# Linear attention, gated feed-forward and residual: more of gate and value in seven half products, attention two blocks ahead

## The chip, the cores and the metric

The kernel runs on one core of a Trainium2 chip. The metric is the device time of one execution in microseconds. TensorE is called PE below, VectorE DVE, ScalarE ACT, GpSimd POOL; SyncE (SP) and POOL issue the transfers.

## The reference

Eight batches of 576 tokens, eight heads of 64. Attention is linear: `kv` is a 64 x 64 matrix per head, and each output row is divided by its root mean square. Its result `x` (4608 x 512) goes through a gated feed-forward layer of 1536 features and is added back under a sigmoid gate.

```python
def _attn_ref(q, k, v, g_norm):
    kv = np.einsum('bhsd,bhse->bhde', k, v)
    out = np.einsum('bhsd,bhde->bhse', q, kv)
    rms = np.sqrt(np.mean(out * out, axis=-1, keepdims=True) + 1e-06)
    return (out / rms * g_norm)

def _moe_ref(x, w_gate, w_val, w_out, w_res):
    gelu = exact_gelu(x @ w_gate)              # written with erf
    ffn_out = gelu * (x @ w_val) @ w_out
    res_gate = 1.0 / (1.0 + np.exp(-(x @ w_res)))
    return x + res_gate * ffn_out
```

## The kernel before

The tokens are worked in nine blocks of 512: blocks 0 to 7 are the first 512 tokens of a batch each, block 8 the remaining 64 of all eight. A block on PE is: gate and value for 12 tiles of 128 features ("slots" 0 to 11), the residual gate (`rps`, 16 matmuls of 512 columns), and the output product, which from block 1 on is done as seven half products (Winograd's form of Strassen's scheme) instead of eight: sums of quarters of `hid` and `w_out` are formed once, seven products of half size are accumulated in PSUM banks A, D, E and F, and some additions put the quarters together. Attention of the next batch is interleaved with the slots.

Gate and value in the plain form, one tile of 128 features: eight matmuls of 512 columns, a GELU on ACT, a product on DVE.

```python
def m_act(blk, f, gps, vps):
    ge = moep.tile([P, NJ * P], FP16, tag="ge", name="ge")
    nc.scalar.activation(out=ge, in_=gps, func=AF.Gelu)
    nc.vector.tensor_tensor(out=hids[blk][:, f, :], in0=ge, in1=vps, op=ALU.mult)

def m_gval(blk, f, pool=pmoe, tag="mm"):
    ...
    m_mm(gps, wg_c, f, blk, 0, NJ)      # four matmuls, 128x512
    m_mm(vps, wv_c, f, blk, 0, NJ)      # four matmuls
    m_act(blk, f, gps, vps)
```

Blocks 7 and 8 have gate and value in sevens too, in three groups of four tiles (`GF = 4`). `gv_group` runs a list of words: a digit is a half product of four matmuls of 256 columns, `E` an ACT copy that seeds bank E from A, `d` an ACT copy of F that is kept, `F` and `c` DVE additions of A and the kept part, `gNN` a GELU and `hNN` the product of a quarter (DVE; quarter 22 on POOL):

```python
for word in """1g 1v Eg 5g Ev 5v dg 6g dv 6v Fg 2g Fv 2v 7g g11 7v cg 3g cv 3v
               h11 g22 4g g12 h12 * 4v g21 h22 h21""".split():
```

It needs four sums of weight quarters for each of gate and value in a group (`weight_sums`), and four sums of token quarters of `xT` per block (`token_sums`), all on DVE. The weight sums are made in blocks 3 to 6, the token sums of blocks 7 and 8 in the output stage of the block before.

The output stage (cut). `aside(...)` marks places where other work may be put in ahead of a product:

```python
def first_two():
    prod(w["A"], a_of(blk, 1, 1), b_of(1, 1), True)
    nc.scalar.copy(out=w["E"], in_=w["A"])
    prod(w["D"], s_[0], wo_t[:, 0], True)
    nc.scalar.copy(out=w["d"], in_=w["D"])
    for j in range(NJ):
        m_sigmoid(j)

def others():
    prod(w["A"], s_[1], wo_t[:, 1], False)
    aside("F")
    sub(nc.vector, w["F"], w["A"], w["d"], ALU.add)
    aside("00")
    prod(w["E"], a_of(blk, 1, 2), b_of(2, 1), False)
    pf((0, 0), w["E"])
    aside("22")
    prod(w["A"], s_[2], wo_t[:, 2], False)
    sub(nc.vector, c22, w["A"], w["d"], ALU.add)
    aside("01")
    prod(w["F"], s_[3], b_of(2, 2), False)
    pf((0, 1), w["F"])                  # pf: DVE, sigmoid times sum
    fin((0, 0))                         # fin: POOL, plus x
    aside("11")
    prod(w["A"], a_of(blk, 2, 2), wo_t[:, 3], False)
    pf((1, 1), c22); pf((1, 0), w["A"])
    ...                                 # more fin, and the stores
```

Attention of a batch b, in short: `by_token` puts q in order (a copy of 128x2048), `d_qT` transposes it by DMA, `a_kv` multiplies k by v (40 small matmuls and a copy), `a_o` makes the output in four banks, `a_rem_o` that of the remaining 64 tokens of two batches (for b = 2, 3, 5, 7), `a_ss` squares on ACT and sums on DVE, `a_norm` makes the inverse root by three Newton steps, `a_t` scales, `a_x` multiplies by g, `d_xT` transposes by DMA. `load_behind` has POOL issue the loads of the next batch after a one-element copy (`hold`) that waits for a transpose. The norm:

```python
def a_norm(b, j0, j1):
    nc.vector.tensor_scalar(out=m, in0=ss, scalar1=1.0 / D, scalar2=RMS_EPS, op0=ALU.mult, op1=ALU.add)
    nc.vector.tensor_scalar(out=yy.bitcast(I32), in0=m.bitcast(I32), ...)
    nc.vector.tensor_scalar(out=mh, in0=m, scalar1=-0.5, scalar2=None, op0=ALU.mult)
    for _ in range(3):
        nc.vector.tensor_tensor(out=a, in0=yy, in1=yy, op=ALU.mult)
        nc.vector.tensor_tensor(out=a, in0=a, in1=mh, op=ALU.mult)
        nc.vector.scalar_tensor_tensor(out=yy, in0=a, scalar=1.5, in1=yy, op0=ALU.add, op1=ALU.mult)
```

Attention of batch b is done in block b - 1 (its q is put in order at the end of block b - 2).

Of the kernel before, what the change touches and what calls it, by code (L numbers as in the profile page):

```python
# [18 lines left out]
def kernel(  # L19
# [91 lines left out]
    def tiles_16(b):  # L111
        b16_t[b, "q"] = qkvp.tile([P, NJ, H, D], FP16, tag="q16", name="q16")
        by_head = [P, H, NJ * D] if b > 0 else [P, NJ, H, D]
        b16_t[b, "k"] = qkvp.tile(by_head, FP16, tag="k16", name="k16")
        b16_t[b, "v"] = qkvp.tile([P, H, NJ * D], FP16, tag="v16", name="v16")
# [10 lines left out]

    def by_token(b):
        nc.vector.tensor_copy(
            out=b16_t[b, "q"].rearrange("p j h d -> p h j d"),
            in_=raw[b, "q"].rearrange("p h (j d) -> p h j d", j=NJ),  # L130
        )
# [66 lines left out]

    def a_kv(b):
        k16 = b16_t[b, "k"]  # L200
        v16 = b16_t[b, "v"]
        kl, vl = last_kv[b % 2]
        ps = pattn.tile([P, NP, D], FP32, tag="at", name="kvp")
        for pr in range(NP):
            for j in range(NJ + 1):
                for e in range(2):
                    h = 2 * pr + e
                    nc.tensor.matmul(  # L208
                        ps[halves(e), pr, :],
                        lhsT=k16[:, h, j * D : (j + 1) * D] if j < NJ else kl[:, h, :],  # L210
                        rhs=v16[:, h, j * D : (j + 1) * D] if j < NJ else vl[:, h, :],
                        start=(j == 0),
                        stop=(j == NJ),
                    )
        nc.vector.tensor_copy(out=st[b]["kv2"], in_=ps)

# [47 lines left out]

    def a_norm(b, j0, j1):

        s = st[b]
        if "rinv" not in s:
            s["rinv"] = attnp.tile([P, NJ + 1, H], FP32, tag="ny", name="ny")
        ss, yy = (t[:, j0:j1, :].rearrange("p j h -> p (j h)") for t in (s["ss"], s["rinv"]))  # L270
        n = (j1 - j0) * H
        m = attnp.tile([P, (NJ + 1) * H], FP32, tag="nm", name="nm")[:, 0:n]
        a = attnp.tile([P, (NJ + 1) * H], FP32, tag="na", name="na")[:, 0:n]
        mh = attnp.tile([P, (NJ + 1) * H], FP32, tag="nh", name="nh")[:, 0:n]
        nc.vector.tensor_scalar(out=m, in0=ss, scalar1=1.0 / D, scalar2=RMS_EPS, op0=ALU.mult, op1=ALU.add)
        nc.vector.tensor_scalar(
            out=yy.bitcast(I32), in0=m.bitcast(I32), scalar1=-0.5, scalar2=float(0x5F3759DF), op0=ALU.mult, op1=ALU.add
        )
        nc.vector.tensor_scalar(out=mh, in0=m, scalar1=-0.5, scalar2=None, op0=ALU.mult)
        for _ in range(3):  # L280
            nc.vector.tensor_tensor(out=a, in0=yy, in1=yy, op=ALU.mult)
            nc.vector.tensor_tensor(out=a, in0=a, in1=mh, op=ALU.mult)
            nc.vector.scalar_tensor_tensor(out=yy, in0=a, scalar=1.5, in1=yy, op0=ALU.add, op1=ALU.mult)

# [176 lines left out]
    def out_by_products(blk, later, banks, amid):  # L461
# [11 lines left out]
        def first_two():  # L473
            for n in ("D", "E", "F", "A"):
                w[n] = pmoe.tile([P, 2, CH], FP32, name="w" + n, bank=banks[n])
            w["d"] = finp.tile([P, 2, CH], FP32, tag="wd", bufs=1, name="wd")
            prod(w["A"], a_of(blk, 1, 1), b_of(1, 1), True)
            nc.scalar.copy(out=w["E"], in_=w["A"])
            prod(w["D"], s_[0], wo_t[:, 0], True)
            nc.scalar.copy(out=w["d"], in_=w["D"])  # L480
            for j in range(NJ):
                m_sigmoid(j)
# [138 lines left out]
    def weight_sums(unit, eng):  # L621
# [4 lines left out]
        def one(s_, x, y, op):  # L626
            if s_ == 0:
                pool, tag = (wpool, f"ws{n}{g}") if g < 2 else (qkvp, "q16")
                gv_sums[unit] = pool.tile([P, 4, 2, 2, P], FP16, tag=tag, name="ws")
# [18 lines left out]
    def token_sums(blk, eng):  # L648
        def one(i, x, y):
            if i == 0:  # L650
                x_sums[blk] = stage.tile([P, 4, 2, 2, P], FP16, tag="qraw", name="ts")
            t = x_sums[blk]
# [9 lines left out]

    def gv_group(blk, g, banks, amid=()):

        if g == 0:
            hids[blk] = hidp.tile([P, NF, NJ * P], FP16, tag="hid", name="hid")
# [63 lines left out]

        for word in """1g 1v Eg 5g Ev 5v dg 6g dv 6v Fg 2g Fv 2v 7g g11 7v cg 3g cv 3v h11 g22 4g g12 h12 * 4v g21 h22 h21""".split():
            if word == "*":
                for f in amid:
                    f()
            elif word[0].isdigit():
                product(int(word[0]), word[1])
# [6 lines left out]
            elif word[0] == "g":  # L743
                gelu(word[1:])
            else:
                hidden(word[1:])

    def out_by_f(blk):
# [338 lines left out]

    def load_behind(b):

        nc.gpsimd.tensor_copy(out=hold, in_=st[b]["qT"][0:1, 0, 0, 0:1])  # L1090
        if pair(b) is not None:
            nc.gpsimd.tensor_copy(out=hold, in_=st[b]["qrT"][0:1, 0, 0:1])
        load_batch(b + 1)

    def at(blk, slot, *fs):
        plans[blk].setdefault(slot, []).extend(fs)

    def plan_attn(b):
# [11 lines left out]
        else:  # L1110
            if b == 3:
                amid_out[m - 1] = {"22": [lambda: by_token(b), *begin]}
            else:
# [19 lines left out]
        last = [lambda: a_t(b, NJ), lambda: a_x(b, NJ), lambda: d_xT(b, NJ, NJ + 1)]  # L1133
        if rem and b + 1 == B:
            amid_out.setdefault(m, {})["F"] = last
        elif rem:
            at(m, NF + 3, *last)

    units = [(n, g) for g in range(NF // GF) for n in "gv"]
    all_sums = [f for u in units for f in weight_sums(u, nc.vector)]  # L1140
    sums_in = {3: all_sums[0:5], 4: all_sums[5:10], 5: all_sums[10:16], 6: all_sums[16:24]}
    SUM_SLOTS = (0, 0, 1, 2, 2, 5, 5, 6)
    out_at = {}

    def banks_of(blk):

        if blk == LAST[0]:
            w = out_at[blk - 1]
            first = {"g": (w["D"], w["F"], w["E"], w["A"]), "v": [w[j] for j in range(NJ)]}
        else:  # L1150
            w = out_at[LAST[0]]
            first = {"g": (w[0], w[2], w["D"], w["A"]), "v": (w[1], w[3], w["E"], w["F"])}
        groups = []
        for g in range(NF // GF):
            groups.append({})
            for u, (a0, e, f, a1) in first.items():
                if g % 2:
                    a0, e, f = a1, f, e
                groups[g].update({(u, "A"): a0, (u, "E"): e, (u, "F"): f})
        (ga0, ge_, gf, ga1), (va0, ve, vf, va1) = first["g"], first["v"]  # L1160
        out_at[blk] = {0: ga1, 1: va1, 2: ge_, 3: ve}
        if blk == LAST[0]:
            out_at[blk].update(A=gf, D=vf, E=ga0, F=va0)
        else:
            out_at[blk].update(A=(gf, vf), D=ga0, E=va0, F=ga1)
        return groups

    late = []
    for blk in range(B + 1):
        plan = plans[blk]  # L1170
        if blk == 0:
# [5 lines left out]
            for b in range(2, B):  # L1177
                plan_attn(b)
            plan[5] = [lambda j=j: a_x(0, j) for j in range(NJ)]
        else:  # L1180
            slots = [lambda f=f: m_gval(blk, f) for f in range(NF)]
            sevens = blk in LAST
            if sevens:
                slots = [None] * NF
                ends = banks_of(blk)
                mid = [lambda: s_begin(blk)]
                for g in range(NF // GF):
                    slots[GF * g] = lambda g=g: gv_group(blk, g, ends[g], mid if g == 2 else ())
            if blk == 1:
# [3 lines left out]
            slots += [lambda i=i: outs[i]() for i in range(4 if blk < B else 2)]  # L1193
            if not sevens:
                plan.setdefault(NFH + 2, []).insert(0, lambda: s_begin(blk))
            for j, f in enumerate(sums_in.get(blk, ())):
                plan.setdefault(SUM_SLOTS[j], []).append(f)
            if blk + 1 in LAST:
                for ahead_of, f in zip(("00", "01", "22", "11"), token_sums(blk + 1, nc.vector)):
                    amid_out.setdefault(blk, {}).setdefault(ahead_of, []).append(f)  # L1200

            def products(blk=blk, outs=outs):
                s_rest(blk)
                if blk not in LAST:
                    out_at[blk] = banks_behind()
                if blk + 1 == LAST[0]:
                    out_at[blk].update({j: pattn.turn[j] for j in range(NJ)})
                if blk < B:
# [11 lines left out]
        if blk == 0:  # L1220
            new_block(1)
            more, rows = attn_plan_1()
            for i, fs in more.items():
                plan.setdefault(i, []).extend(fs)
        elif blk + 1 < B:
            new_block(blk + 1)
# [43 lines left out]
```

## Time and profile before

| | |
|---|---|
| time, median of 3 | 335.93 us (335.91 to 335.99) |
| span of the profiled execution | 334.7 us |
| granted TensorE clock | 0.999 |
| plain tile of gate or value, 4 matmuls of 512 | 0.86 us |
| half product of gate or value, 4 matmuls of 256 | 0.44 us |
| half product of the output stage, 12 matmuls of 256 | 1.31 us |
| block 3, 4, 5, 6 | 34.89, 35.29, 34.88, 35.30 us |
| block 7 (sevens, no attention) | 30.97 us |

Busy time is the time in which an engine has an instruction at work; it can include waiting that the record doesn't separate. In the chain of waits, each row is a start, a duration and the work that held the end at that moment. In the timelines, a row is an instruction or a run of equal ones; a bracket says how long the engine was idle before it and what ended the idleness. The records of successive DVE operations overlap by a little under 0.1 us, so the spacing of starts is shorter than the durations.

### The profile page before, as it was taken

How to read it: one execution, taken by the hardware profiler on the slowest of the kernel's cores; microseconds unless marked ns; L12 is line 12 of the kernel's file. 1: busy time of each engine (PE TensorE's matmuls, PEld its weight loads, DVE VectorE, ACT ScalarE, POOL GpSimd, SP SyncE). 2: the span in 40 equal slices, each digit the busy share in tenths (PEclk: the TensorE clock that was granted, in tenths of full speed). 3: DMA queues.
4: the chain of work that ended last, by engine and by line, in shares of the span. 5: the costliest groups of instructions: out<-in, count | busy, mean ns of one | idle time of the engine just before them, and what ended most of it. 6: DMA issues, size and time to landing. Idle time of an engine off the chain costs nothing.

```text
span 334.7 us, 6522 instructions
## 1 busy us (share of the span) xinstructions
PE 326.6 (98%) x2576; PEld 201.4 (60%) x2576; DVE 253.5 (76%) x498; ACT 161.5 (48%) x290; POOL 109.3 (33%) x127
## 2 busy tenths in 40 slices
PE   8999999999999999999999999999999999999993
PEld 3554454445844485447644664467445888788872
DVE  6755459579867979697778978795799877687754
ACT  3663474374336352636173525343544376646660
POOL 2882242980064018200830066004100241142232
PEclk9999999999999999999999999999999999999999
DMA  7999999689589284965496349935201330011004
GB/s 258 314 204 203 195 203 159 163 122 132 98 130 206 65 127 131 167 58 108 158 151 67 63 127 179 114 63 102 107 0 20 60 126 2 2 63 66 0 2 125
DMA packets 76688, 38.82 MB, mean 116 GB/s; under 512 B 42098, under 2 KB 74354, under 8 KB 76658
## 3 DMA queue, kind: packets, MB, share of 16 engines
q0 software_dynamic: 38752, 17.17, 40.9%
q1 hardware_dynamic: 37328, 20.71, 23.6%
q10 hardware_dynamic: 578, 0.52, 0.5%
q8 instruction: 20, 0.33, 0.4%
q14 instruction: 10, 0.08, 0.1%
HBM read 38.80 MB, written 9.44 MB: 144 GB/s over the span
## 4 chain that ended last, share of the span: by engine, by line
PE 96%; DVE 2%; issue 0%; DVEq 0%
PE gps L357 22%; PE vps L357 21%; PE wA L452 11%; PE rps L377 9%; PE fps L394 3%; PE Av L692 3%; PE Ag L692 3%; PE wF L452 3%; PE wE L452 3%; PE wD L452 3%; PE w L452 2%; PE idle L858 2%; PE kvp L208 2%; PE Fv L692 2%; PE Fg L692 2%; PE op L226 1%
## 5 line engine op out<-in xcount | busy, mean ns | idle before, releaser
L345 ACT ACTIVATE ge<-gps 128x512 f16<-128x512 f32 x84 | 50.0, 598 | 97.4 <-PE gps L357 96.4
L357 PE MATMUL gps<-xT,wg 128*128 128x512 f16 x328 | 84.3, 380 | 0.0
L357 PE MATMUL vps<-xT,wv 128*128 128x512 f16 x328 | 84.2, 379 | 0.0
L346 DVE TENSOR_TENSOR hid<-ge,vps 128x512 f16<-128x512 f16 x84 | 57.3, 684 | 33.0 <-PE vps L357 30.9
L492 POOL TENSOR_TENSOR osb<-osb,t 128x512 f32<-128x512 f32 x28 | 35.2, 1275 | 136.5 <-DVE osb L488 136.1
L357 PEld LDWEIGHTS <-wv 128*128 128x128 f16 x328 | 32.1, 98 | 38.7
L357 PEld LDWEIGHTS <-wg 128*128 128x128 f16 x328 | 30.7, 98 | 34.6 <-issue 0.2
L452 PEld LDWEIGHTS <-hid_s 128*128 128x128 f16 x384 | 37.6, 98 | 4.5 <-issue 0.2
L377 PE MATMUL rps<-wr,xT 128*128 128x512 f16 x144 | 32.5, 379 | 0.0
L452 PEld LDWEIGHTS <-hid 128*128 128x128 f16 x288 | 28.1, 98 | 5.2 <-issue 0.6
L386 ACT ACTIVATE th<-rps 128x512 f32<-128x512 f32 x36 | 21.5, 598 | 16.4 <-PE rps L377 16.4
L377 PEld LDWEIGHTS <-xT 128*128 128x128 f16 x144 | 14.1, 98 | 16.5
L245 DVE TENSOR_REDUCE ss<-sq 128x8 f32<-128x512 f32 x32 | 20.6, 680 | 2.9 <-ACT sq L243 2.7
L452 PE MATMUL wA<-wo_ts,hid_s 128*128 128x256 f16 x168 | 20.6, 272 | 0.0
L692 PEld LDWEIGHTS <-ws 128*128 128x128 f16 x192 | 18.8, 98 | 2.2
L391 ACT ACTIVATE th<-th 128x512 f32<-128x512 f32 x36 | 19.9, 622 | 0.0
L303 DVE TENSOR_TENSOR t<-op,ny 128x512 f16<-128x512 f32 x28 | 17.9, 684 | 0.1
L243 ACT ACTIVATE sq<-op 128x512 f32<-128x512 f32 x28 | 15.3, 596 | 4.5 <-PE op L226 4.1
L425 DVE TENSOR_TENSOR hid_s<-hid 128x1536 f16<-128x1536 f16 x16 | 15.3, 954 | 0.2
L317 DVE TENSOR_TENSOR t<-t,g 128x512 f16<-128x512 f16 x36 | 15.0, 468 | 0.1
L729 POOL TENSOR_TENSOR hid<-ge,c 128x512 f16<-128x512 f16 x6 | 7.0, 1166 | 23.4 <-ACT ge L723 23.4
L394 PE MATMUL fps<-wo,hid 128*128 128x512 f16 x48 | 11.2, 379 | 0.0
(173 smaller groups left out, 472.8 us busy)
## 6 DMA issues: line engine op xcount, KB each, us to landing
out_dram<-osb SPq DMA_DIRECT2D x14, 512.0 KB, 2.6
qraw<-in_q_dram POOLq DMA_DIRECT2D x7, 512.0 KB, 8.3
k<-in_k_dram POOLq DMA_DIRECT2D x7, 512.0 KB, 9.7
v<-in_v_dram POOLq DMA_DIRECT2D x7, 512.0 KB, 11.9
wg<-in_moe_w_gate_dram POOLq DMA_DIRECT2D x2, 512.0 KB, 8.3
wv<-in_moe_w_val_dram POOLq DMA_DIRECT2D x2, 512.0 KB, 8.7
wo<-in_moe_w_out_dram POOLq DMA_DIRECT2D x2, 512.0 KB, 13.7
out_dram<-osb SPq DMA_DIRECT2D x4, 256.0 KB, 2.8
```

The lines of the kernel that those rows point to most:

```text
L245: nc.vector.tensor_reduce(out=out_, in_=sq, op=ALU.add, axis=mybir.AxisListType.X)
L303: nc.vector.tensor_tensor(out=t, in0=o, in1=scale, op=ALU.mult)
L345: nc.scalar.activation(out=ge, in_=gps, func=AF.Gelu)
L346: nc.vector.tensor_tensor(out=hids[blk][:, f, :], in0=ge, in1=vps, op=ALU.mult)
L357: nc.tensor.matmul(ps[:, j0 * P : j1 * P], lhsT=w[:, cc, :], rhs=xT_t[blk][:, j0:j1, cc, :], start=(cc == 0 and j0 == 0), stop=(cc == NP - ...
L377: nc.tensor.matmul(rps, lhsT=xT_t[blk][:, j, cc, :], rhs=wr16[:, cc, :], start=(cc == 0), stop=(cc == NP - 1),)
L386: nc.scalar.activation(out=th, in_=rps, func=AF.Tanh, scale=0.5)
L391: nc.scalar.activation(out=th, in_=th, func=AF.Copy, scale=0.5, bias=0.5)
L394: nc.tensor.matmul(fps, lhsT=hids[blk][:, f, j * P : (j + 1) * P], rhs=wo16[:, f, :], start=(f == 0), stop=(f == NF - 1))
L452: nc.tensor.matmul(ps[:, e - es[0], :], lhsT=a[:, f, e * P : (e + 1) * P], rhs=b[:, f, :], start=(start and e == es[0] and f == 0), stop=( ...
L492: nc.gpsimd.tensor_tensor(out=res_all[of], in0=res_all[of], in1=t_t[blk][of], op=ALU.add)
L692: nc.tensor.matmul(out_[:, r, :], lhsT=lhsT, rhs=rhs, start=(first and r == 0 and c == 0), stop=(c == 1), skip_group_check=True,)
```

## The change

In blocks 3 to 6 the last two of the three groups of gate and value (tiles 4 to 11) are done in sevens, and the first stays plain. Its purpose is to take one product in eight out of two thirds of these blocks' gate and value work on PE. What has to move for it:

- Attention of batches 4 to 7 goes two blocks ahead, so that its work is spread over the end of one block and the plain group of the next, and so that banks of PSUM are free for the groups.
- q's copy and kv's copy go from DVE to ACT, and the norm of these batches to POOL, where each Newton step has four operations for three (fifteen in all for twelve).
- The weight sums of groups 1 and 2 are made in block 0, and those of group 0 in block 6 (blocks 7 and 8 need them). Token sums are made for blocks 3 to 8.
- The banks that gate and value use rotate with those of attention (`banks_of`).

The diff, cut to its core:

```diff
-    def by_token(b):
-        nc.vector.tensor_copy(
+    def by_token(b, copy=nc.vector.tensor_copy, js=slice(0, NJ)):
+        copy(
...
-    def a_norm(b, j0, j1):
+    def a_norm(b, j0, j1, eng=nc.vector):
...
-            nc.vector.scalar_tensor_tensor(out=yy, in0=a, scalar=1.5, in1=yy, op0=ALU.add, op1=ALU.mult)
+            if eng is nc.vector:
+                eng.scalar_tensor_tensor(out=yy, in0=a, scalar=1.5, in1=yy, op0=ALU.add, op1=ALU.mult)
+            else:
+                eng.tensor_scalar(out=a, in0=a, scalar1=1.5, scalar2=None, op0=ALU.add)
+                eng.tensor_tensor(out=yy, in0=a, in1=yy, op=ALU.mult)
...
             nc.scalar.copy(out=w["E"], in_=w["A"])
+            aside("D")
             prod(w["D"], s_[0], wo_t[:, 0], True)
             nc.scalar.copy(out=w["d"], in_=w["D"])
+            aside("gates")
...
-    def load_behind(b):
+    def load_behind(b, x_of=None):
         nc.gpsimd.tensor_copy(out=hold, in_=st[b]["qT"][0:1, 0, 0, 0:1])
+        if x_of is not None:
+            nc.gpsimd.tensor_copy(out=hold, in_=xT_t[x_of][0:1, 0, 0, 0:1])
...
+    GROUPS = {blk: (1, 2) for blk in range(3, B - 1)} | {B - 1: (1, 0, 2), B: (0, 1, 2)}
+    def plan_attn_ahead(b):
+        rem = pair(b) is not None
+        m = b - 2
+        act, pool = nc.scalar.copy, nc.gpsimd
...
+        if m in GROUPS:
+            for i in range(2):
+                at(m, 2 + i, lambda i=i: by_token(b, act, slice(2 * i, 2 * i + 2)))
+            at(m, 3, *begin)
+            if b + 1 < B:
+                at(m, 2 * GF, lambda: load_behind(b))
+            at_word(m, 1, "5v", lambda: a_kv(b, act))
+        else:
+            at(m, 5, lambda: by_token(b, act, slice(0, 2)))
+            at(m, 6, lambda: by_token(b, act, slice(2, 4)))
+            at(m, 7, *begin)
+            at(m, NF - 1, lambda: a_kv(b, act))
+            at(m, NF, lambda: load_behind(b, b - 1))
+        if rem:
+            at_word(m, 1, "h21", lambda: a_rem_o(b))
+        at(m, NF, lambda: a_o(b), lambda: a_ss(b, 0), lambda: a_ss(b, 1))
+        aside_out(m, "D", lambda: a_ss(b, 2), lambda: a_ss(b, 3))
+        aside_out(m, "gates", *[lambda: a_ss(b, NJ)] * rem, lambda: a_norm(b, 0, NJ + rem, pool))
+        at(m, NF + 3, lambda: new_block(b), lambda: a_t(b, 0), lambda: a_t(b, 1))
+        for j in range(2, NJ + rem):
+            at(m + 1, j - 2, lambda j=j: a_t(b, j))
+        for j in range(NJ):
+            at(m + 1, 2 + j // 2, lambda j=j: a_x(b, j))
+        at(m + 1, 3, lambda: d_xT(b, 0, NJ))
+        if rem:
+            at(m + 1, 3, lambda: a_x(b, NJ), lambda: d_xT(b, NJ, NJ + 1))
+
+    units = [(n, g) for g in (1, 2, 0) for n in "gv"]
+    sums = {u: weight_sums(u, nc.vector) for u in units}
+    for slot, u in ((6, ("g", 1)), (8, ("v", 1)), (11, ("g", 2)), (13, ("v", 2))):
+        for i in range(2):
+            at(0, slot + i, *sums[u][2 * i : 2 * i + 2])
+    late_sums = [f for u in (("g", 0), ("v", 0)) for f in sums[u]]
+    at(B - 2, NF + 1, *late_sums[0:4])
+    for key, f in zip(("00", "22", "01", "11"), late_sums[4:8]):
+        aside_out(B - 2, key, f)
+    for blk in GROUPS:
+        t = token_sums(blk, nc.vector)
+        if blk - 1 in GROUPS and blk < B:
+            at(blk - 1, NF + 1, *t)
+        else:
+            for key, f in zip(("00", "01", "22", "11"), t):
+                aside_out(blk - 1, key, f)
...
```

## The prediction

> **What bounds the kernel now.** I read the page's busy shares first, then the busy time by block, then the chain of waits, and then the timelines of VectorE (DVE) and GpSimd (POOL) around two transitions. The shares say that TensorE (PE) never rests:
>
> ```profile
> PE 326.6 (98%) x2576; PEld 201.4 (60%) x2576; DVE 253.5 (76%) x498; ACT 161.5 (48%) x290; POOL 109.3 (33%) x127
> ```
>
> By block (3, 4, 5, 6 and 7 in turn; the columns are length, then busy time of each engine with its instructions):
>
> ```profile
> 126.95:161.84 34.89, 34.89 (x270) 20.27 (x268) 29.11 (x61) 14.87 (x26) 10.44 (x12) 1.00 0.75 120
> 161.84:197.13 35.29, 35.29 (x285) 20.36 (x284) 28.00 (x58) 16.08 (x29) 10.19 (x13) 1.00 0.67 111
> 197.13:232.01 34.88, 34.88 (x270) 20.26 (x268) 29.02 (x57) 14.87 (x26) 10.55 (x12) 1.00 0.73 120
> 232.01:267.31 35.30, 35.30 (x287) 20.40 (x285) 30.23 (x63) 16.07 (x29) 5.04 (x5) 1.00 0.17 49
> 267.31:298.28 30.97, 30.97 (x271) 26.23 (x269) 23.35 (x36) 18.41 (x34) 8.33 (x8) 1.00 0.09 35
> ```
>
> PE's busy time is the whole of every block: there is no wait to remove, only PE work. Block 7 already has gate and value in seven half products and no attention, and VectorE works 23 of its 31 us. The chain gives the price of both forms:
>
> ```profile
> 21.49 0.86 PE gps L357 x4
> 22.35 0.86 PE vps L357 x4
> ...
> 267.31 0.44 PE Ag L692 x4
> 267.75 0.44 PE Av L692 x4
> ...
> 285.65 3.45 PE rps L377 x16
> ```
>
> A plain tile of 128 features costs 0.864 for gate and 0.864 for value: four tiles are 6.91 us. Block 7's three groups in sevens run from 267.31 to 285.65, 18.34 us, so 6.11 each. One changed group saves 0.80 us.
>
> **What the Trainium skill says.** "TensorE: Matmul & The Clock Gate", Back-to-back issue gap, has 518 cycles for 512 columns and 262 for 256 in its table; at its 2.4 GHz I estimate 216 and 109 ns. The trace agrees: 0.864/4 is 216 ns, and a 256-column matmul takes 0.437/4, 109 ns. Half products thus lose almost nothing by being smaller. (The 131 ns for N=512 in the same section isn't seen here.) "SBUF — State Buffer", Who interferes with whom, says that a VectorE operation with both inputs in SBUF and a GpSimd operation that reads SBUF exclude each other for a whole instruction. The trace agrees: the gated product of two SBUF tiles took 1.65 us at 297.94, beside a POOL addition from 297.77 to 299.04, and 0.68 us at 231.34. "PSUM — Partial Sum Buffer", PSUM bank collisions raise a hardware error, wants engines kept apart by bank: so a product that accumulates into bank A starts only when VectorE has read A. The wait lists have no PE entry for it; after the change there may be one.
>
> **The change part by part.** (1) *Sevens.* Four blocks of two groups, eight groups: each drops 32 matmuls of 512 columns and adds 56 of 256, in all 192 matmuls more. 8 x 0.80 = 6.4 us off the path. The floor is 335.9 - 6.4 = 329.5.
>
> (2) *VectorE.* A group in sevens costs it four additions and three products, about 0.69 each, 4.8 us; four plain products cost 4 x 0.684 = 2.7. Eight times 2.1 is +16.6. Token sums for four more blocks: 16 x 0.435 = +7.0. Gone: four norms of 12 small operations (about 2.3 each, -9.2), four casts of q (0.69 each, -2.7) and of kv (0.42, -1.7). Net +10, so about 263 us. The weight sums only move, two thirds of them to block 0, where the waits on "PE vps" show VectorE idle 1.0 us per tile; the last eight go into block 6.
>
> (3) *ScalarE (ACT).* A group goes from 4 x 0.60 to eight operations of 0.57 to 0.63, +2.4, in all +19. The q copies, two of 1024 elements per batch, cost 1.02 us each (by the row of 128x1024, 1019 ns), +8; kv +1.5. About 190 us, off the path.
>
> (4) *POOL.* One product of 1.17 per group, +9.4, and four norms of 15 dependent small operations. The page has only the 1x1 copies, 0.18 to 0.25 us; I estimate 0.3 for 32 to 40 elements from these and the 1.2 us of 512 elements, 4.5 us a norm, +18. About 137 us.
>
> (5) *Attention two blocks ahead.* The same PE work at other places: block 2 carries two batches (1.5 us more), block 6 none. PE sum unchanged.
>
> **Where the gain leaks.** PE ends a block's output stage by a chain through VectorE. Before, the addition into F has slack; here it is in block 7, with the VectorE operation ahead of it:
>
> ```profile
> 289.49 0.96 DVE L425 TENSOR_TENSOR hid_s<-hid,hid_s 128x1536 f16<-128x1536 f16 x1
> 293.14 0.70 DVE L425 TENSOR_TENSOR wF<-wA,wd 128x512 f32<-128x512 f32 x1 [2.70 <-PE wA L452]
> ```
>
> The group ended at 285.65, so VectorE is free 4.75 us later (290.4). The changed order puts ahead of that addition five sums of squares in blocks 3 and 5 (four in block 4) and four token sums. The timelines show starts 0.60 apart for operations that read 0.68, and 0.34 to 0.45 for token sums: 3.0 + 1.6, so the addition starts at 9.35 and has read bank A at 10.0. PE wants A for the fifth product at 0.38 (remainder rows) + 3.45 (gate) + 0.69 (output of attention) + 4 x 1.31 = 9.76. A wait of some 0.3 in blocks 3 and 5, 0.1 in block 4. In block 6, eight weight sums of half size (about 0.23 each) and the token sums delay it to about 8.8 against 8.7 (0.15), and further weight sums sit ahead of the later read of A, beside POOL's additions with their lock: another 0.6. Sum of the four output stages: 1.45.
>
> Block 3's start is worse. In block 2, POOL's loads now wait for the transpose of block 3's activations as well:
>
> ```profile
> 117.12 2.00 SPq L334 DMA_TRANSPOSE xT<-t  x1
> ...
> 130.98 0.93 POOL L120 DMA_DIRECT2D qraw<-in_q_dram  x1
> 131.90 0.89 POOL L121 DMA_DIRECT2D k<-in_k_dram  x1
> 132.78 0.90 POOL L122 DMA_DIRECT2D v<-in_v_dram  x1
> ```
>
> That transpose starts at 117.1 and lands 4.5 later (median of its row), 121.7. Two copies and six load issues (130.98 to 135.72 in this instance, 4.7 us) take POOL to 127.0; the norm behind them ends at 131.5. Block 3 starts on PE at 126.95 + 1.5 = 128.5, and VectorE's first operation there, the scaling of attention, waits for that norm; the first hidden product sits behind two scalings and ends at 133.4. PE needs its bank for the third value tile at 128.5 + 4.32 = 132.8. A wait of 0.6, and about 0.4 more where `t` times `g` meets POOL's late additions: 1.0. In blocks 4 to 6 POOL starts the norm at 9.4 after the group end and ends near 13.9; the scaling comes at about 15, so no wait.
>
> Last, the copy of kv on ACT between the seed and the kept sums of the third group: kv is ready about 3.3 into the group, the copy takes 0.4, the two kept sums then end at 4.85, and the two VectorE additions after them at 5.7; PE wants the second at 5.5. 0.15 in three blocks, 0.4 together.
>
> Sum: 329.5 + 1.45 + 1.0 + 0.4 = 332.4. I take 332.2.
>
> **The rivals.** *A: all is hidden.* PE runs through and the time is 329.6. For it: block 7 has sevens with no PE wait and VectorE has 7 us to spare there. Against: blocks 3 to 5 add attention's 8 or 9 us to that. *B: VectorE becomes the bound.* By rows, a changed block with remainder has 2.7 (plain) + 9.6 (groups) + 3.8 (hidden sums) + 4.1 (output) + 3.4 (squares) + 3.4 (scalings) + 2.2 (`g`) + 1.7 (token sums) = 30.9, of 33.3 that PE needs. By the starts' spacing it is nearer 28. On average it fits, but if waits on POOL or port locks cost 2 us a block the whole gain goes: 335 to 337. *C: GpSimd's norm is slow.* At 0.5 us for a small operation a norm takes 7.5 us: block 3's start loses 3 us more and blocks 4 to 6 begin to lose 1 to 2 each: 337 to 340. "GPSIMD Engine Reference", 3.1 Elementwise, has GpSimd at about 1.96 times VectorE's time; the trace has 1.16 to 1.27 against 0.68, about 1.8, and VectorE's small ones at 0.18 to 0.20 would give 0.35: so C isn't likely at its full size. *D: transfers come late.* Batch 4's q was issued at 95.06 with 6.0 us to land, and ACT reads it at about 104: hidden.
>
> **Range and chances.** The floor is firm, since PE's work is counted: under 329.5 nothing is to be had, and 2% (329.2) lies just beyond it, so faster by 2% has 0.02. My leaks could be zero or twice as big, and B or C in part add 2 or 3 us: 330.0 to 335.2. Slower by 2% (342.6) would need 13 us of waits, 0.03.
>
> **What would show it right or wrong.** Right: PE busy falls by about 6.4 us with 2768 matmuls; new PE idle or stretched pieces of 0.1 to 0.7 at the fifth product of the output stages and about 1 us in block 3's second or third tile; VectorE near 263, ACT 190, POOL 137 us; block 7 still 31.0. Wrong: a seven group longer than 6.2 without a wait, POOL's small operations far from 0.3, PE waiting for ACT in the groups, or VectorE without gaps through blocks 3 to 5.

## The result, and the profile after

The changed kernel takes 333.09 us (333.05 to 333.13) where the kernel before takes 335.96 us (335.91 to 336.47) beside it: a ratio of 0.9911, with a 95% interval of 0.9894 to 0.9928. It is faster by 2.9 us of the 6.4 us of matmuls that it leaves out. The question for the experiments is where the other 3.5 us went.

The page's busy shares, as before:

```profile
PE 320.6 (97%) x2768; PEld 219.6 (66%) x2768; DVE 258.7 (78%) x482; ACT 184.6 (56%) x334; POOL 133.9 (40%) x196
```

PE has the 2768 matmuls that were counted. It is busy for 6.0 us less, and no longer for the whole span. By block (3, 4, 5, 6 and 7 in turn, from each block's first gate matmul; after the length come the busy times of PE, its weight loads, VectorE, ScalarE and GpSimd, then the granted clock, the DMA share and GB/s):

```profile
128.46:163.65 35.19, 34.13 (x335) 25.05 (x333) 27.61 (x46) 21.89 (x40) 18.87 (x37) 1.00 1.05 146
163.65:197.10 33.45, 33.45 (x319) 24.93 (x317) 27.74 (x47) 20.62 (x37) 16.87 (x30) 1.00 0.71 120
197.10:231.56 34.46, 33.97 (x335) 25.05 (x333) 27.68 (x46) 21.90 (x40) 10.96 (x21) 1.00 0.31 68
231.56:263.68 32.12, 31.93 (x247) 23.85 (x245) 28.78 (x58) 16.56 (x30) 9.10 (x11) 1.00 0.19 54
263.68:294.64 30.96, 30.96 (x271) 26.22 (x268) 23.50 (x37) 18.39 (x34) 8.24 (x8) 1.00 0.09 35
```

Length minus PE's busy time is 1.06, 0.00, 0.49, 0.19 and 0.00 us: the new waits are in blocks 3, 5 and 6. VectorE has at least 3 us free in every block, also in those. PE's timeline names the waits (start, duration, instructions, and in the bracket the idle time before them and what ended it):

```profile
91.22 1.04 PE L361 MATMUL gps<-xT,wg 128*128 128x512 f16 x4 [0.33 <-DMA xT<-t]
...
124.54 1.47 PE L456 MATMUL wA<-wo_ts,hid_s 128*128 128x256 f16 x12 [0.30 <-DVE wF L429]
...
131.92 1.03 PE L361 MATMUL gps<-xT,wg 128*128 128x512 f16 x4
133.80 1.02 PE L361 MATMUL vps<-xT,wv 128*128 128x512 f16 x4 [0.86 <-DVE hid L350]
...
146.85 0.60 PE L698 MATMUL Ag<-ts,ws 128*128 128x256 f16 x4
147.45 0.60 PE L698 MATMUL Av<-ts,ws 128*128 128x256 f16 x4
...
158.05 1.47 PE L456 MATMUL wE<-wo,hid 128*128 128x256 f16 x12
159.72 1.47 PE L456 MATMUL wA<-wo_ts,hid_s 128*128 128x256 f16 x12 [0.20 <-DVE wF L429]
...
227.63 1.47 PE L456 MATMUL wA<-wo_ts,hid_s 128*128 128x256 f16 x12 [0.49 <-DVE wF L429]
262.37 1.47 PE L456 MATMUL wA<-wo_ts,hid 128*128 128x256 f16 x12 [0.19 <-DVE osb L429]
```

The brackets must not be taken for the loss. Four 256-column matmuls read 0.60 us, but the next four start 0.43 or 0.44 later: the recorded end lies 0.16 us behind the moment at which the next could begin. A delay therefore costs its bracket plus 0.16, and a short one has no bracket at all: from 146.85 to 147.45 the spacing is 0.60 where 0.44 is due, and nothing shows; a delay of 0.27 us in run 10 shows nothing either. In what follows a *loss* is the spacing of two starts minus the number of matmuls times 216 ns (512 columns) or 109 ns (256 columns). For 131.92 to 133.80 it is 1.88 - 0.86 = 1.02 us.

Added up over blocks 2 to 6 (the joints with attention's small matmuls, about 0.1 each and present before too, are left out). The fifth of the seven output products is the one with `s_[2]`; it can go into bank A only when the addition into F has read it. In block 6 the loss is at the seventh.

| place | predicted | before | after |
|---|---|---|---|
| block 2, first gate tile (transfer of its activations) | none | 0.06 | 0.50 |
| block 2, fifth output product | none | 0 | 0.47 |
| block 3, start | 1.0 | 0 | 1.02 |
| kv copy, blocks 3, 4 and 5 | 0.4 | 0 | 0.46 |
| block 3, fifth output product | 0.3 | 0 | 0.36 |
| block 4, fifth output product | 0.1 | 0 | 0 |
| block 5, fifth output product | 0.3 | 0 | 0.66 |
| block 6, output stage | 0.75 | 0 | 0.36 |
| sum | 2.85 | 0.06 | 3.83 |

335.96 - 6.4 + 3.77 = 333.3, within 0.3 us of the measured time. The six named places give 2.86 us; block 2 was named nowhere and gives 0.91 more. For comparison, the fifth product of block 2 in the kernel before follows the fourth at 1.31 us:

```profile
121.55 1.47 PE L452 MATMUL wE<-wo,hid 128*128 128x256 f16 x12
122.86 1.47 PE L452 MATMUL wA<-wo_ts,hid_s 128*128 128x256 f16 x12
```

### The profile page after: what moved, and what is told of

It is laid out like the page before. It is cut to its first block, busy times and chain, and to the rows that moved or that the text cites. A ratio compares the mean times of both kernels' runs of the same rounds, so it can differ in the third digit from the quotient of the medians.

```text
span 331.3 us, 7035 instructions
## 1 busy us (share of the span) xinstructions
PE 320.6 (97%) x2768; PEld 219.6 (66%) x2768; DVE 258.7 (78%) x482; ACT 184.6 (56%) x334; POOL 133.9 (40%) x196
## 4 chain that ended last, share of the span: by engine, by line
PE 88%; DVE 4%; DMA 3%; SPq 1%; ACT 1%; issue 1%; POOL 0%; DVEq 0%; ACTq 0%
PE vps L361 13%; PE gps L361 13%; PE rps L381 10%; PE wA L456 9%; PE Av L698 8%; PE Ag L698 7%; PE Fv L698 4%; PE Fg L698 4%; PE fps L398 3%; PE w L456 2%; PE wD L456 2%; PE wF L456 2%; PE wE L456 2%; PE Ev L698 2%; PE Eg L698 2%; PE kvp L208 2%
## 5 line engine op out<-in xcount | busy, mean ns | idle before, releaser
L349 ACT ACTIVATE ge<-gps 128x512 f16<-128x512 f32 x52 | 30.8, 597 | 64.6 <-PE gps L361 64.3
L361 PE MATMUL vps<-xT,wv 128*128 128x512 f16 x200 | 51.3, 379 | 0.9 <-DVE hid L350 0.9
L361 PE MATMUL gps<-xT,wg 128*128 128x512 f16 x200 | 51.4, 379 | 0.3 <-DMA xT<-t 0.3
L350 DVE TENSOR_TENSOR hid<-ge,vps 128x512 f16<-128x512 f16 x52 | 35.4, 683 | 20.0 <-PE vps L361 17.5
L698 PEld LDWEIGHTS <-ws 128*128 128x128 f16 x448 | 43.6, 98 | 5.6 <-issue 0.5
L735 POOL TENSOR_TENSOR hid<-ge,c 128x512 f16<-128x512 f16 x14 | 16.3, 1163 | 73.1 <-ACT ge L729 73.1
L361 PEld LDWEIGHTS <-wv 128*128 128x128 f16 x200 | 19.6, 98 | 24.6 <-issue 1.1
L361 PEld LDWEIGHTS <-wg 128*128 128x128 f16 x200 | 19.0, 98 | 21.8 <-DMA xT<-t 0.6
L719 DVE TENSOR_TENSOR Fg<-Ag,d 128x512 f32<-128x512 f32 x14 | 9.8, 700 | 16.2 <-PE Ag L698 9.0
L698 PEld LDWEIGHTS <-wg 128*128 128x128 f16 x168 | 16.4, 98 | 2.7
L698 PEld LDWEIGHTS <-wv 128*128 128x128 f16 x168 | 16.4, 98 | 1.9
L698 PE MATMUL Ag<-ts,ws 128*128 128x256 f16 x112 | 16.8, 273 | 0.0
```

What stands on the lines that cost most here:

```text
L361: nc.tensor.matmul(ps[:, j0 * P : j1 * P], lhsT=w[:, cc, :], rhs=xT_t[blk][:, j0:j1, cc, :], start=(cc == 0 and j0 == 0), stop=(cc == NP - ...
L698: nc.tensor.matmul(out_[:, r, :], lhsT=lhsT, rhs=rhs, start=(first and r == 0 and c == 0), stop=(c == 1), skip_group_check=True,)
L735: eng.tensor_tensor(out=dst, in0=ge[q], in1=source(q, "v"), op=ALU.mult)
```

## The experiments

The theory: each loss is a matter of order, an operation standing ahead of the one that PE needs on VectorE, ScalarE or GpSimd. The rivals: VectorE is full and any order costs the same; or the move of attention, the norm on GpSimd or the held loads cost time in some other way. Each run has the kernel before beside it, at 335.9 to 336.1 us. Every diff is against the changed kernel. Executions differ by up to 0.8 us in what lies ahead of block 1, which starts between 55.3 and 56.1 us in the traces, so small effects are read from the lengths of the blocks.

**1. All six loads behind the norm.** In block 2, GpSimd issues batch 5's loads ahead of batch 4's norm.

```diff
-            at(m, NF, lambda: load_behind(b, b - 1))
+            aside_out(m, "F", lambda: load_behind(b, b - 1))
```

> The loads of batch 5, which POOL issues in block 2 ahead of batch 4's norm, are issued behind that norm. Theory (the gain leaks at single places where one instruction stands in the wrong order): the norm starts when its sums are ready, near 121.8 us, and ends 5.3 later at about 127; the wait of 0.86 us at the third value tile of block 3 goes, and the time falls by 0.8 to 0.9, to about 332.2. Batch 5's q lands about 133, just ahead of ACT's copy at 134. Rival (VectorE is the bound through blocks 2 to 5): the wait only moves to the next place, a group's additions or the output stage of block 3, and the time stays at 333.1 within 0.2. Second rival (the loads were early for a reason): ACT's copy of q waits and holds a GELU up, and the time rises by 1 or more.

Measured: 336.21 us (335.62 to 338.09), ratio 1.0006 (0.9995 to 1.0017). The theory's number is missed by 4 us, and the second rival is right. Block 3's wait did go: the norm ended at 129.46 us, not 131.83. Two new waits came. ScalarE has batch 5's q to copy, which is now loaded later, and sits still until it lands; and the loads delay GpSimd's additions into the time when VectorE multiplies by g. From the timelines of this kernel, ScalarE's, GpSimd's and VectorE's lines:

```profile
136.19 1.04 ACT L128 COPY q<-qraw 128x1024 f16<-128x1024 f16 x1 [2.24 <-DMA qraw<-in_q_dram]
...
140.63 0.57 ACT L708 COPY Ev<-Av 128x512 f32<-128x512 f32 x1 [1.48 <-DVE hid L350]
```

```profile
134.92 4.74 POOL L498 TENSOR_TENSOR osb<-osb,t 128x512 f32<-128x512 f32 x4
```

```profile
134.88 5.06 DVE L321 TENSOR_TENSOR t<-t,g 128x512 f16<-128x512 f16 x2
```

VectorE's two operations take 5.06 us where 0.84 is usual. The first takes 3.77 us, until the third of GpSimd's four additions is over; the second gets in beside the fourth and takes 1.37 us. The hidden product behind them comes late. PE pays twice, first for ScalarE's late copy of q, which stands ahead of the seed Eg, then for VectorE's hidden product, for which the seed Ev waits. PE's brackets there are 1.55 us for Eg and 1.46 for Ev, 3.3 us of losses. Behind them PE ran at half its clock (third column from the right: 0.50; four matmuls took 0.85 us for 0.44), which cost 1.6 us more:

```profile
141.70:144.70 3.00, 3.00 (x16) 2.06 (x14) 1.47 (x3) 1.09 (x3) 0.00 (x0) 0.50 1.50 312
```

The traced execution took 337.34 us. Of the 22 executions, ten with a mean clock of 0.99 took 336.8 to 338.1 us, and twelve with 0.995 or more took 335.6 to 336.2.

"SBUF — State Buffer", Who interferes with whom, in the Trainium skill, speaks of an exclusive lock for one instruction; here one VectorE operation was kept out over three GpSimd instructions in a row. So the loads can't all stand between the norm and the additions: q's is needed early, and together they push the additions into VectorE's multiplications.

**2. The hold on the activations' transpose left out.** The loads are issued as soon as q's transpose allows.

```diff
-            at(m, NF, lambda: load_behind(b, b - 1))
+            at(m, NF, lambda: load_behind(b))
```

> In block 2 POOL no longer waits for the transpose of block 3's activations ahead of the loads of batch 5: the loads are issued from about 112 us on instead of 121.7, still ahead of the norm of batch 4. Theory (the wait at block 3's start is the norm's place behind the loads, and e1 failed because it pushed the loads and POOL's additions into block 3): the norm starts at about 122.5, when its sums are ready, and ends near 127.8, POOL's four additions are over by 132.5, before VectorE multiplies by g at 134; the wait of 0.86 us goes and nothing else moves: 332.2 to 332.3. Rival (the hold protects the transpose): the loads slow it from 4.5 us to 8 or more, the token sums of block 3 are late on VectorE, and the time stays or rises by up to 1.

Measured: 337.22 us (335.52 to 338.94), ratio 1.0039 (1.0025 to 1.0052). The rival is right in its mechanism, and had the loss too small (up to 1 us). The transpose of block 3's activations, issued at 116.81, now shares its time with the loads, and VectorE waits for it until 128.90, 12.1 us later (4.3 is the median of its row in the changed kernel). VectorE's line:

```profile
128.90 0.42 DVE L429 TENSOR_TENSOR ts<-xT 128x512 f16<-128x512 f16 x1 [4.38 <-DMA xT<-t]
```

PE's last product of the block then has a bracket of 3.56 us:

```profile
130.91 2.10 PE L456 MATMUL wA<-wo_ts,hid 128*128 128x256 f16 x12 [3.56 <-DVE osb L429]
```

The loss there is 3.7 us, for the 1.0 that block 3's start no longer loses, and again PE ran at half clock behind it (0.50 from 131.6 to 134.6 us), some 1.6 us more. The four executions with a mean clock of 0.995 took 335.5 to 336.0 us, the other eighteen, with 0.992 or less, 337.1 to 338.9.

The hold, which with the six issues behind it costs block 3 a microsecond, is what makes the change pay: without it the kernel is no faster than before.

**3. The loads split.** Between the two failures lies this one: q, k and v stay ahead of the norm, the last 64 tokens' three small loads go behind the additions.

```diff
+        if not split:
+            load_rest(b)
+
+    def load_rest(b):
         load_last_kv(b)
...
-        load_batch(b + 1)
+        load_batch(b + 1, split=x_of is not None)
...
             at(m, NF, lambda: load_behind(b, b - 1))
+            at(m, NF + 3, lambda: load_rest(b + 1))
```

> Of batch 5's six loads, which GpSimd issues ahead of the norm in the output stage of block 2, only the three large ones (q, k and v of the first 512 tokens) stay there; the three small ones (the last 64 tokens' q, k and v) come after the block's last four additions. My theory is that block 3's wait of 0.86 us is nothing but these six issues standing ahead of the norm: three of them last 0.71 to 0.73 us, so the norm should start about 2.1 us earlier (near 124.4 us) and end near 129.8 us, the wait of the value product on the VectorE (0.86 us) goes, no other wait comes, batch 5's q is there in time since its load is issued as before, and the time is about 332.2 us (332.0 to 332.5), 0.3% under the change's. Rival: the GpSimd's four back-to-back additions, which then run from about 129.8 to 134.3 us, meet the VectorE's float16 multiplications by g at about 134 us and hold them up (5.06 us for one of them in the kernel that moved all six loads), and the time stays at 333 us or goes above it.

Measured: 332.37 us (332.03 to 332.71), ratio 0.989 (0.9869 to 0.991). GpSimd's timeline (line numbers are four higher in this kernel): the norm starts at 124.47 and ends at 130.20, then come the additions, then the small loads.

```profile
124.47 0.44 POOL L279 TENSOR_SCALAR nm<-ss 128x32 f32<-128x32 f32 x1
...
130.16 4.50 POOL L502 TENSOR_TENSOR osb<-osb,t 128x512 f32<-128x512 f32 x4
134.60 0.77 POOL L109 DMA_DIRECT2D kl<-in_k_dram  x1
```

Block 3 takes 34.16 us for 35.19, 1.03 us less, where the ledger has 1.02 for its start; the other blocks keep their lengths to within 0.02. (By the medians the gain over the change is 0.7 us, and the two intervals overlap; the reading rests on block 3.) To move three of the six load issues is enough to take the loss at block 3's start away.

**4. Token sums spread.** Those of blocks 4, 5 and 6 stand ahead of the addition into F; here they go one by one between the output products.

```diff
-        if blk - 1 in GROUPS and blk < B:
-            at(blk - 1, NF + 1, *t)
-        else:
-            for key, f in zip(("00", "01", "22", "11"), t):
-                aside_out(blk - 1, key, f)
+        for key, f in zip(("00", "01", "22", "11"), t):
+            aside_out(blk - 1, key, f)
```

> In blocks 3 to 6 the four token sums of the next block stand between the products of the output stage, as in blocks 2 and 7, and not all ahead of the addition into F. Theory: that addition starts 1.5 us earlier on VectorE, the waits of the fifth product in blocks 3 and 5 (0.20 and 0.49 us) go, nothing else moves: about 332.4. Rival (VectorE is the bound): the 1.5 us reappear later, as a wait for bank A of the last product or at the next block's first tiles, and the time stays at 333.1 or rises; in block 6, where weight sums stand at the same places, it may rise by 0.5.

Measured: 333.86 us (333.27 to 333.92), ratio 0.992 (0.9904 to 0.9936): no gain. The loss at the fifth product falls from 0.36 to 0.27 in block 3 and from 0.66 to 0.27 in block 5, but in block 6 the token sums now stand among the weight sums, beside GpSimd's additions with their lock, and the loss there doubles from 0.36 to 0.72; block 7 is 0.20 us longer as well. Blocks 3 to 7 together are as long as in the changed kernel, to within 0.1 us; the rest of the 0.8 us lies ahead of block 1. The line of VectorE in this kernel:

```profile
261.00 1.38 DVE L429 TENSOR_TENSOR ts<-xT 128x512 f16<-128x512 f16 x1
```

That operation takes 0.42 us elsewhere. Half the theory stands: order decides where the time is lost.

**5. The copy of kv on VectorE.**

```diff
-            at_word(m, 1, "5v", lambda: a_kv(b, act))
+            at_word(m, 1, "5v", lambda: a_kv(b))
```

> kv's copy of batches 4 to 7 is on VectorE again and not on ACT. Theory: in the third group VectorE sits idle 2.4 us before its first addition, waiting for ACT's kept sum, which the copy of 0.37 us delays; without the copy the kept sums end 0.3 earlier, and PE's stretch of 0.15 us at 6v of 7g 7v goes in blocks 3, 4 and 5: 0.4 us less, about 332.7. Rival (VectorE is the bound, and the copy was moved to relieve it): 0.42 us more of VectorE work in each of four blocks makes the time rise by 0.5 to 1.5.

Measured: 333.12 us (333.01 to 333.71), ratio 0.9907 (0.989 to 0.9925): the same. The stretch of 0.15 is gone from all three blocks, but PE reaches the fifth output product sooner by just that and waits there: the loss rises from 0.36 to 0.53 in block 3 and from 0.66 to 0.74 in block 5. Only block 4, which has no such wait, is shorter (33.38 for 33.45). A loss upstream of a longer wait is not worth its length.

**6. The multiplication by g left out.** Batches 4 to 7 are not multiplied by g, so this output lacks that factor.

```diff
-            at(m + 1, 2 + j // 2, lambda j=j: a_x(b, j))
+            pass
...
-            at(m + 1, 3, lambda: a_x(b, NJ), lambda: d_xT(b, NJ, NJ + 1))
+            at(m + 1, 3, lambda: d_xT(b, NJ, NJ + 1))
```

> Batches 4 to 7 leave out the multiplication of x by g (the output is then without g there): 1.4 to 1.8 us of VectorE work less in the plain group of each of blocks 3 to 6. Theory (VectorE has slack there, the waits lie in the output stages and at block 3's start, ahead of this work): within 0.2 of the changed kernel's 333.1. Rival (VectorE is the bound through blocks 3 to 6): 1 us or more less.

Measured: 333.41 us (333.33 to 334.45), ratio 0.993 (0.9917 to 0.9943). VectorE does 6.0 us less (252.7 for 258.7), and every wait is as it was (0.30, 0.87, 0.20 and 0.47 us). In this trace block 1 starts 0.34 us later than in the changed kernel's, and that is the 0.3 us by which it took longer. Work taken from VectorE away from the waited-for chain gains nothing, so VectorE as a whole is not the bound.

**7. The norm on VectorE.**

```diff
-lambda: a_norm(b, 0, NJ + rem, pool))
+lambda: a_norm(b, 0, NJ + rem))
```

> Batches 4 to 7 have their norm on VectorE again, at the same place in the program: that one part of the change undone. Theory: 2.3 us of small operations stand ahead of the addition into F in the output stages of blocks 2, 3, 4 and 5; the waits there grow from 0.30, 0.20, 0 and 0.49 us by 2.2 each (block 4 by about 2.0), while block 3's start loses its 0.86: about +8 us, 340 to 342. Rival (POOL's norm is a cost, because its small operations take 1.5 times as long and hold up the scaling): the time falls by up to 1 us, or stays.

Measured: 347.19 us (346.51 to 349.1), ratio 1.0331 (1.0304 to 1.0359), 6 us above what I expected. Here the same engine's total is again small (268.3 us), but the norm's twelve small operations lie in the chain ahead of the addition into F. A line of PE's timeline:

```profile
165.94 2.72 PE L456 MATMUL wA<-wo_ts,hid_s 128*128 128x256 f16 x12 [2.75 <-DVE wF L429]
```

That is block 3; from block 2 to 5 the brackets are 3.24, 2.75, 2.24 and 2.76 us. As losses they are 11.6 together, for 1.5 in the changed kernel, and block 3's start has none: 9.1 us more. The other 5 us are slower matmuls behind three of the waits (the first twelve take 2.44 to 2.72 us for 1.47); the last section comes back to it. GpSimd's norm is worth about 14 us to this change.

**8. Attention two blocks ahead, without the sevens in blocks 3 to 6.**

```diff
-    GROUPS = {blk: (1, 2) for blk in range(3, B - 1)} | {B - 1: (1, 0, 2), B: (0, 1, 2)}
+    GROUPS = {B - 1: (1, 0, 2), B: (0, 1, 2)}
+    AHEAD = range(3, B + 1)
...
-            at_word(m, 1, "h21", lambda: a_rem_o(b))
+            at(m, NF - 1, lambda: a_rem_o(b))
...
-                (plan_attn if b - 1 not in GROUPS else plan_attn_ahead)(b)
+                (plan_attn if b - 1 not in AHEAD else plan_attn_ahead)(b)
```

> The other part of the change alone: attention two blocks ahead with its copies on ACT and its norm on POOL, the weight sums in block 0 and 6, but gate and value of blocks 3 to 6 in plain form as before (PE's matmuls are those of the kernel before). Theory (sevens are the only gain, attention ahead only costs): the waits of block 2 (0.3 + 0.3) and of block 3's start (0.9) stay, those of the output stages go as there are no token sums: 336.5 to 337.5. Rival (moving work from VectorE to ACT and POOL is itself worth something): 335.9 or less.

Measured: 340.34 us (340.01 to 340.53), ratio 1.0131 (1.0116 to 1.0146). It is 3 us above what I expected. Its output differs from the reference's by 2.5%, for a reason that stays open; it has the 2576 matmuls of the kernel before, and I read its time alone, with that caution.

PE's timeline:

```profile
124.79 1.47 PE L456 MATMUL wA<-wo_ts,hid_s 128*128 128x256 f16 x12 [0.31 <-DVE wF L429]
134.09 1.02 PE L361 MATMUL vps<-xT,wv 128*128 128x512 f16 x4 [0.90 <-DVE hid L350]
151.88 0.32 PE L254 MATMUL orp<-kv,qrT 64*64 64x64 f16 x15 [0.33 <-ACT kv L215]
```

The move alone costs some 4.4 us. The losses of block 2 (0.44 and 0.47) and of block 3's start (1.06) are there at their full size without a single new seven; the fifth products of blocks 3 and 5 lose 0.27 each, and block 6 loses 0.81, with its token sums spread as in run 4. About 1 us of the 4.4 is of my making: the remainder's product stands right behind kv's copy and waits 0.33 and 0.32 us, with 0.16 more each. So some 2.5 of the change's 3.8 us belong to moving attention. The sevens add the copy of kv inside a group (0.46) and what the token sums cost at the fifth products (0.48).

**9. The orders together, without the hold.** Token sums spread over the output stages of blocks 3 to 5 alone (block 6 keeps its weight sums clear), kv's copy on VectorE, the last scaling of batch 3 behind the addition into F, and no hold.

```diff
-            at(m, NF, lambda: load_behind(b, b - 1))
+            at(m, NF, lambda: load_behind(b))
...
-            aside_out(m, "F", *last)
+            aside_out(m, "00", *last)
...
-            at_word(m, 1, "5v", lambda: a_kv(b, act))
+            at_word(m, 1, "5v", lambda: a_kv(b))
...
-        if blk - 1 in GROUPS and blk < B:
+        if blk == B - 1:
```

> Four orders at once: no wait of the loads for the transpose (as the run above), token sums spread over the output stage in blocks 3, 4 and 5 but not in 6, batch 3's last scaling in block 2 behind the addition into F, and kv's copy on VectorE. Theory (single places, each with its own price): 0.86 + 0.30 (block 2) + about 0.5 (blocks 3 and 5, as the token sums' run had it by block) + 0.2 to 0.4 (kv, whose wait no longer comes back because the additions into F have slack): 1.9 to 2.1 less than the changed kernel, 331.0 to 331.3. Rival (VectorE is the bound in these blocks): waits come back elsewhere and less than 1 us is gained.

Measured: 338.61 us (338.52 to 338.95), ratio 1.0079 (1.0067 to 1.0091). That is 7 us above what I expected. As in run 2, the transpose comes late, here with a wait of 5.29 us in block 2 and half the clock behind it (0.50 from 133.0 to 136.0 us). But blocks 3 to 6 take 34.34, 33.30, 33.91 and 32.11 us for 35.19, 33.45, 34.46 and 32.12: no fifth product has a bracket any more. Block 3's start has no loss either, but that is not the orders' doing: without the hold the norm is early. What the orders are worth together, run 10 tells.

**10. The split loads and the orders.** Run 3 and the last three edits of run 9.

> The same split of the loads, and with it three orders on the VectorE: the sums of the tokens for blocks 4 to 6 spread over the output stage ahead of each (as blocks 3 and 7 have them), the last scaling of batch 3 one product later, and the copies of kv of batches 5, 6 and 7 on the VectorE for the ScalarE. If the waits of the output stages (0.30, 0.20 and 0.49 us in blocks 2, 3 and 5), the stretch of the kv products (0.15 us in three blocks) and block 3's wait (0.86 us) are each a matter of order alone, blocks 3 to 6 take about 34.3, 33.3, 33.9 and 32.1 us, as in the kernel that had these orders without the hold on xT, and the time is 331.0 us (330.7 to 331.6). Rival: as with each of these orders alone, a wait that goes comes back in the next place where the chain of the VectorE meets a product (the lock beside GpSimd's additions in block 6 above all), and the time is 332.2 us or more, no better than the split alone.

Measured: 330.83 us (330.8 to 331.7), ratio 0.9847 (0.9828 to 0.9866), clear of the change's interval: the fastest version, 5.1 us under the kernel before. On top of run 3 the three orders are worth 1.3 us by the lengths of blocks 2 to 5 (1.5 by the medians). Two of them, tried alone in runs 4 and 5, were worth nothing: kv's copy because the fifth products took most of it back, the token sums because blocks 6 and 7 lost what blocks 3 and 5 gained (block 6 is left out here). One bracket is left from block 2 to block 5 (0.31, block 2's transfer), and the loss at the fifth product of block 3 is too short to have one:

```profile
156.50 1.47 PE L460 MATMUL wE<-wo,hid 128*128 128x256 f16 x12
158.07 1.47 PE L460 MATMUL wA<-wo_ts,hid_s 128*128 128x256 f16 x12
```

Its losses at the table's places are 0.48, 0, 0.06, 0, 0.26, 0, 0.27 and 0.36, together 1.43 us. 335.9 - 6.4 + 1.37 = 330.9. The ledger closes for this kernel as for the change.

## Why the prediction was right, point by point

- *The sevens.* 2768 matmuls, 8 x 0.80 us off PE's work, block 7 unchanged at 30.96: right. Inside the groups PE waits at one place alone, behind the copy of kv. The wait for bank A to be read, which the prediction kept in mind, shows there (VectorE has read it at 147.40, PE starts at 147.45) and at the fifth output products.
- *The engines' totals.* VectorE 258.7 (263 predicted), ScalarE 184.6 (190), GpSimd 133.9 (137): right to 3%, though VectorE rose by 5 us and not by 10. Run 6 shows that such totals say little here: 6 us of VectorE fewer, the same time. Rival B is out.
- *Block 3's start.* 1.0 predicted, 1.02 measured, 1.03 given back when the load issues are moved (run 3). The sum was right by luck, since two errors cancel: no port lock took 0.4 there (the multiplications by g took 0.84 us for two). The norm was longer than estimated: 15 operations from 126.49 to 131.83, 5.3 us where I took 4.5, so the first hidden product came 0.35 us later than predicted. Rival C was right in direction, at a small part of its size.

```profile
126.49 0.21 POOL L275 TENSOR_SCALAR nm<-ss 128x32 f32<-128x32 f32 x1
...
131.58 0.25 POOL L287 TENSOR_TENSOR ny<-na,ny 128x32 f32<-128x32 f32 x1
```

- *The kv copy.* 0.4 predicted, 0.46 measured. It was right as a loss, but run 5 shows that it could not be had by itself.
- *The output stages.* 1.45 predicted, 1.38 measured, again with luck: block 5 lost 0.36 more than predicted and block 6 lost 0.39 less. In block 5 a sum ahead of the addition into F took 1.25 us for 0.95, beside a product on GpSimd from 216.91 to 218.08; that is the 0.30 by which it loses more than block 3. In block 6 I had put 0.6 on the weight sums beside the lock; the lock is there (1.46 us for two sums at 260.25, beside a GpSimd addition from 260.41 to 261.56), but the reader of bank A was only 0.36 late. VectorE's sum in block 5:

```profile
217.64 1.25 DVE L429 TENSOR_TENSOR hid_s<-hid 128x1536 f16<-128x1536 f16 x1
```

- *The step that failed: the list of places.* "Sum of the four output stages" counted blocks 3 to 6, and the start of block 3, and left out block 2, where batch 4's attention now lies beside batch 3's. There the last scaling of batch 3 (0.68) and its multiplication by g (0.43) stand ahead of the addition into F, behind the four sums of squares of batch 4. The change itself moved the two (`last` in `plan_attn`): before, they came at the end of the block. VectorE's timeline after:

```profile
122.73 0.68 DVE L307 TENSOR_TENSOR t<-o,ny 128x512 f16<-128x512 f32 x1
123.45 0.43 DVE L321 TENSOR_TENSOR t<-t,g 128x512 f16<-128x512 f16 x1
123.79 0.69 DVE L429 TENSOR_TENSOR wF<-wA,wd 128x512 f32<-128x512 f32 x1
```

and before:

```profile
121.82 0.70 DVE L425 TENSOR_TENSOR wF<-wA,wd 128x512 f32<-128x512 f32 x1 [0.67 <-PE wA L452]
...
127.60 0.94 DVE L303 TENSOR_TENSOR t<-o,ny 128x512 f16<-128x512 f32 x1
```

Put behind that addition (run 10), they let it start at 123.03, and the 0.47 us is gone:

```profile
123.03 0.70 DVE L433 TENSOR_TENSOR wF<-wA,wd 128x512 f32<-128x512 f32 x1 [0.21 <-PE wA L460]
```

The other 0.44 (0.50 against 0.06) is the transpose of block 2's activations. Issued at 86.28, it is awaited until 91.22, 4.94 us; before it was 86.98 to 91.48, 4.50 us. All ten of the kernels above have it (0.47 to 0.53). What slows it was not separated and stays open. These 0.91 us are about the distance between the predicted 332.2 and the measured 333.1 (the working's own sum was 332.4, and was taken 0.2 lower).

Rival A (all hidden, 329.6) was out of reach for the order as written, yet run 10 comes within 1.3 us of it. Rival D, late transfers, didn't come for q's loads, but runs 1 and 2 show how near it was: with another order a load or a transpose does come late.

## What to carry to other kernels

When an engine never rests and a change takes work from it, list every place at which it takes something from another engine, in the blocks next to the changed ones too, and work out at each which operation stands last ahead of the one it needs; engine totals don't tell. Measure losses by the spacing of starts, not by idle brackets, and test orders together: one that gains nothing alone can be upstream of another wait. A load's issue is an operation on its engine, and moving it can trade its own wait for a transfer that collides or a lock that bites.

## What the runs showed of the hardware that I had not expected

- *A wait can cost more than its length.* In run 7, the 3 us behind the waits of blocks 3 and 5 (the windows of this kernel; the granted clock is the third column from the right):

```profile
166.00:169.00 3.00, 3.00 (x16) 2.08 (x16) 0.78 (x2) 0.00 (x0) 1.15 (x1) 0.53 1.07 70
241.50:244.50 3.00, 3.00 (x28) 2.69 (x28) 1.41 (x3) 0.00 (x0) 1.15 (x1) 1.00 0.00 0
```

After the 2.75 us of block 3 TensorE had about half its clock (16 matmuls in 3 us, for 28), as after those of blocks 2 and 4 (0.56 and 0.50); after the 2.76 us of block 5 it had all of it. "TensorE: Matmul & The Clock Gate", Part 1: The HAM clock gate, says that the clock is halved after an idle window of some 3.4 us, and that the windows run freely. The halving agrees, and so does the luck in it: in run 1 ten of the 22 executions have the lower mean clock. Shorter waits than that page's window were enough here, 2.24 us in block 4, and in run 1 1.55 and 1.46 us with four matmuls between them. Each time the clock stayed at half for 3.4 us, which costs 1.7 us of PE's work. Waits of up to 0.86 us in the changed kernel left the clock at 1.00.
- *GpSimd's small operations.* On 128x32 elements they read 0.21 to 0.48 us and follow each other, each needing the one before, at 0.36 us on average (5.3 us for 15); VectorE's like operations read 0.20.
- *The lock over a series.* A VectorE multiplication of 0.42 us took 3.77 us beside three GpSimd additions in a row, and the next one 1.37 us beside the fourth (run 1).
